# First batch of a pooled attention: half of v loaded in rows of eight tokens and summed by GpSimd instead of TensorE

## The chip, the cores and the metric

The kernel runs on one core of one Trainium2 chip. The metric is the device time of one execution in microseconds (us). Lower is better. The engines are named as in the profile: PE is TensorE (PEld its weight loads), DVE is VectorE, ACT is ScalarE, POOL is GpSimd, SP is SyncE, which here only issues transfers (DMAs). A q behind the name is the engine's sequencer, which waits and issues.

## The reference

Eight batches of attention with eight heads, 576 tokens and 64 columns a head. Keys and values are first averaged over groups of eight tokens, so that 576 queries meet 72 keys. The result of all heads, 4608 rows of 512, goes through a two-layer network with 2048 hidden columns:

```python
k_p = k.reshape(B, H, Sp, pool, D).mean(axis=3)
v_p = v.reshape(B, H, Sp, pool, D).mean(axis=3)
scores = scale * np.matmul(q, k_p.transpose(0, 1, 3, 2))
scores = scores - np.max(scores, axis=-1, keepdims=True)
attn = np.exp(scores)
attn = attn / (np.sum(attn, axis=-1, keepdims=True) + 1e-09)
attn_out = np.matmul(attn, v_p)
...
h = x @ w_in                      # x: attn_out as 4608 x 512
s = np.sin(alpha * h)
g = h + s * s / (alpha + 1e-09)
out = g @ w_out
```

All inputs and the output are float32.

## The kernel before

**Stages.** Both matrix products of the network are done by a fast scheme with seven block products in place of eight (combinations of blocks of w_in and of x are formed first, products p = 1 to 7 follow, and sums put them together). The first layer runs over nine units `u` of 512 rows. Each unit is 28 slots: four groups `J` of seven products, one product a slot (`hidden`, L834, in groups of eight matmuls of 128x256). Its result g goes to a DRAM buffer. The second layer (`outputs`, L1312) reads it back.

**What runs beside it.** `carry(u)` puts the attention of batch u + 1 and other work into the slots of unit u by hand, as a list of functions for each slot. The engines work in the order in which the instructions are written; there is no planner. A DMA issued on SyncE waits in SyncE's own order too, and its rows queue behind those of the DMAs issued earlier.

**The first batch** has its own code (`first_batch`, L1061 and on). Nothing covers it, so the loads of k, q, v and w_in are issued in the order of need, and the sums over eight tokens are split between engines:

- k (`load_k_heads`): four tokens lie in a row; VectorE or GpSimd adds the two halves of a row, and TensorE multiplies by a matrix of ones (`twos`) that also adds and transposes (L374).
- v (`load_v_rows`): heads 0 to 7 lie in a tile `h` of 128 partitions, four tokens of a head to a row of 1 KB, loaded in two DMAs of four heads (L184). `sum_v_rows(b, g, i)` sums heads 4g to 4g + 3 on TensorE: sixteen matmuls with `twos` (L203) into PSUM bank i, and ScalarE copies the result to the tile `vm` (L204). The last 64 tokens of each head are a small DMA of their own (L182), summed with `eights` (L193).
- `a_head(g, ...)` transposes the normalised weights of heads 4g to 4g + 3 on TensorE (L466, L474). `norm_head(hp, eng)` makes them for two heads: a sum and a reciprocal on VectorE (L432, L433), and two multiplications on `eng` (L438). `values` multiplies weights and v (L556, L558), ScalarE scales the result into x (L527) and VectorE forms the first two differences that the fast scheme wants (L567).
- `root` takes an approximate square root for the factor c of s * s; `refine` is one step of refinement, four operations on 128x16 (L644, L645). Squares use c (L991).
- `combine_w_in(J, steps, eng)` forms the combinations of w_in's blocks for group J (L675): step 0 is s1 = a21 + a22, step 1 is s2 = s1 - a11, steps 2 and 3 follow.

Later batches load v otherwise (`load_v`, L140): rows of eight tokens, 2 KB each, heads 0 to 3 into partitions 0 to 63 and heads 4 to 7 into 64 to 127, and GpSimd sums them by halving a row three times (`pool_rows`, L131).

**Order around the change.** In `first_batch` the DMAs on SyncE stand in this order: alternating heads of k and q, v's last tokens, v of heads 0 to 3, v of heads 4 to 7, q of heads 6 and 7, four blocks of w_in (L669), q's last tokens (L101), batch 1's k (L121) and q (L84, L101). Unit 0 follows, with w_in's blocks for groups 1 to 3 in slot 2 and batch 1's v in slot 7. A DMA's completion semaphore comes from a ring of eight, so each issue also waits for the landing of the one eight before it. In slot 1 of unit 0, v of heads 4 to 7 is summed (`sum_v_rows(0, 1, 2)`), q's last tokens are transposed (`rest_q`, L399, into the PSUM bank from which L567 has read) and `a_head(1)` follows; slot 2 has `values` for heads 4 to 7. Batch 1's weights are divided by GpSimd (`norm`, L365), transposed by VectorE (`turn`, L491, L494), and the sums of unit 0 (`hidden`'s adds, L809 and L1036) stand between them in VectorE's order.

Of the kernel before, what the change touches and what calls it, by code (L numbers as in the profile page):

```python
# [19 lines left out]
P = 128  # L20
POOL = 8
# [19 lines left out]
class Kernel:  # L41
# [137 lines left out]
    def load_v_rows(self, b, main, rest):  # L179

        self.v_rows = main.rearrange("p (h t d) -> p h t d", h=self.H, t=4), rest[:64].rearrange("p (h d) -> p h d", h=self.H)
        self.nc.sync.dma_start(out=self.v_rows[1], in_=self.v[b, :, 4 * P:, :].rearrange("h p d -> p h d"))  # L182
        for h in range(0, self.H, 4):
            self.nc.sync.dma_start(out=self.v_rows[0][:, h:h + 4].rearrange("p h t d -> p h (t d)"),  # L184
                                   in_=self.v[b, h:h + 4, 0:4 * P, :].rearrange("h (p t) d -> p h (t d)", t=4))
        self.vp[b] = self.ap.tile([P, self.H // 2, self.D], F32, name="vm", bufs=2), self.ap.tile([P, self.H // 2, self.D], F32, name="vz", bufs=2)

    def sum_v_rest(self, b, i):

        nc = self.nc  # L190
        ps = self.psum([P, 2, self.D], i)
        for hp in range(4):
            nc.tensor.matmul(ps[32 * hp:32 * hp + 32], self.eights[:], self.v_rows[1][:, 2 * hp:2 * hp + 2], start=True, stop=True)  # L193
        nc.vector.tensor_tensor(out=self.vp[b][1][:, 0:2], in0=ps, in1=self.mask[:, 0:2].unsqueeze(2).to_broadcast([P, 2, self.D]), op=OP.mult)
# [866 lines left out]
    def first_batch(self):  # L1061

        nc = self.nc
        self.att = [self.attention(b) for b in range(self.B)]
        A = self.att[0]

        far = [self.home(i, [P, 4 * POOL * self.D]) for i in (1, 2)]
        h = [self.hp.tile([P, 4 * POOL * self.D], F32, name="h") for _ in range(2)]
        self.k_rows = far[0][:].rearrange("p (h t d) -> p h t d", h=self.H, t=4)
        self.k_sums = far[1][:, 0:1024].rearrange("p (h u d) -> p h u d", h=self.H, u=2)  # L1070
        self.new_q(0)
        self.load_alpha(self.hp.tile([P, P], F32, name="s", bufs=1)[:])
        self.load_q_heads(0, 0, 2, nc.scalar)
        add_k = [self.load_k_heads(0, nc.sync, nc.vector)]
        add_rest = self.load_k_rest(h[1][:, 576:832], far[1][:, 1024:1152])
        one = self.sm.tile([P, 1], F32, name="one")
        nc.scalar.activation(out=one[:], in_=self.ident[:, 0:1], func=AF.Sqrt)

        def fill(n):

            for _ in range(n):
                nc.tensor.matmul(self.psum([P, 4, P], 4), self.full[:], self.full[:].unsqueeze(1).to_broadcast([P, 4, P]), start=True, stop=True)
        fill(5)
        self.turn_alpha()
        refine = self.root()
        nc.scalar.activation(out=one[:], in_=one[:], func=AF.Exp)
        add_k[0]()
        tr = self.new_tr()
        nc.gpsimd.memset(tr[:, 2048:], 0.0)
        self.a0 = tr[:, 0:2048].rearrange("p (t j s k) -> p t j s k", t=4, j=4, s=2)  # L1090
        self.z0 = tr[:, 2048:2560].rearrange("p (t hp x k) -> p t hp x k", t=4, hp=4, x=4)
        self.kb2 = h[1][:, 0:self.H * self.Sp].rearrange("p (h k) -> p h k", h=self.H)
        self.a4 = self.last[:64, 0:512].rearrange("p (j s k) -> p j s k", j=4, s=2)
        self.z4 = self.last[:64, 512:640].rearrange("p (hp x k) -> p hp x k", hp=4, x=4)
        nc.gpsimd.memset(self.z4, 0.0)
        for hp in range(1, 4):
            add_k.append(self.load_k_heads(hp, nc.sync, nc.vector if hp < 2 else nc.gpsimd))
            if hp < 3:
                self.load_q_heads(0, 2 * hp, 2 * hp + 2)
        self.load_v_rows(0, h[0][:], self.tp.tile([P, self.DM], F32, name="p5")[:])  # L1100
        self.load_q_heads(0, 6, 8)
        self.load_w_in()
        self.load_w_in_part(0)
        self.q_rest = self.A[3][:64, 0, 512:1024].rearrange("p (h d) -> p h d", h=self.H)
        A.new_a()
        fill(4)
        A.k_head(0)
        add_rest()
        A.q_head(0)
        A.k_last()  # L1110
        for f in add_k[1:]:
            f()
        fill(1)
        A.products_head(0)
        A.q_head(1)
        A.k_head(1)
        A.soft_shift(0)
        A.soft_exp(0)
        fill(1)
        A.products_head(1)  # L1120
        A.k_head(2)
        A.q_head(2)
        A.soft_shift(1)
        A.soft_exp(1)
        A.norm_head(0, nc.gpsimd)
        A.norm_head(1, nc.vector)
        fill(2)
        A.products_head(2)
        self.sum_v_rest(0, 0)
        self.sum_v_rows(0, 0, 3)  # L1130
        A.k_head(3)
        A.q_head(3)
        A.soft_shift(2)
        A.a_head(0, (1, 7, 0), (0,))
        self.combine_w_in(0, (0,), nc.gpsimd)
        A.products_head(3)
        A.a_head(0, (1, 7, 0), (1,))
        A.soft_exp(2)
        A.soft_shift(3)
        A.norm_head(2, nc.gpsimd)  # L1140
        A.soft_exp(3)
        A.norm_head(3, nc.gpsimd)
        self.combine_w_in(0, (1,))
        self.combine_w_in(0, (2, 3), nc.gpsimd)
        A.values((0, 1), (5, 6), 2, 0)
        refine()
        self.load_q_rest(0, self.q_rest)
        for e in range(2):
            self.load_k(1, e)
            self.pool_k[e]()  # L1150
        self.load_q(1)
        self.load_w_in_part(1)

    def carry(self, u):

        nc = self.nc
        x = defaultdict(list)
        at = lambda slot, f, *a: x[slot].append(lambda: f(*a))
        last = self.B - 1
        b = u + 1  # L1160
        if u == 0:
            A0, A = self.att[:2]
            at(1, self.sum_v_rows, 0, 1, 2)
            at(1, A0.rest_q)
            at(1, A0.a_head, 1, (5, 7, 2))
            at(2, A0.values, (2, 3), (2, 1), 1, 1)
            at(2, A0.score, 4)
            at(2, self.sums_of_x, 0, 2)
            at(2, self.sums_of_x, 0, 3)
            at(2, self.load_w_in_part, 2)  # L1170
            at(2, self.load_w_in_part, 3)
            at(2, self.pairs_q, 1, range(5))
            at(4, self.combine_w_in, 1, (0, 1, 2, 3), self.nc.gpsimd)
            at(4, A.q_t, 0, self.nc.vector.tensor_copy)
            at(4, A.q_t, 1, self.nc.vector.tensor_copy)
            at(4, A.k_t)
            at(7, self.load_v, 1)
            at(7, lambda: self.pool_v())
            for i in range(2):
                at((5, 10)[i], A.two_scores, i)  # L1180
            at(13, A.two_shifts)
            for i in range(2, 5):
                at(5 + i, A.q_t, i)
            at(9, A0.exp, 4)
            for i in range(4):
                at((9, 9, 15, 15)[i], A.exp, i)
                at((10, 10, 16, 16)[i], A.norm, i)
                at((13, 13, 17, 19)[i], A.turn, i)
            at(8, self.combine_w_in, 2, (0, 1, 2, 3), self.nc.gpsimd)
            at(13, A0.norm_rest)  # L1190
            at(17, self.combine_w_in, 3, (0, 1), self.nc.gpsimd)
            at(17, self.combine_w_in, 3, (2, 3), self.nc.gpsimd)
            at(23, A0.a_rest)
            at(24, lambda: A0.values_rest((5, 6, 7, (self.turn + 1) % 5)))
            for r in (32, 96):
                at(3, self.nc.gpsimd.memset, self.aM[r:r + 32, :, 704:736], 0.0)
            at(19, A.move, range(3))
            at(20, A.move, (3,), nc.scalar, (0,))
            at(21, A.move, (3,), nc.scalar, (1,))
            at(26, A.all_values)  # L1200
            at(9, self.load_q, 2)
            at(23, self.inner_w_in)
            for e in range(2):
                at(12, self.load_k, 2, e)
                at(17, lambda e=e: self.pool_k[e]())
            at(27, self.att[2].k_t)
            turn = 23
        else:
            at(0, self.sums_of_x, u, 2)
            at(0, self.sums_of_x, u, 3)  # L1210
        if 0 < u < last:
            A = self.att[b]
# [366 lines left out]
```

## Time and profile before

| | before |
|---|---|
| time of a run, median of 3 (lowest to highest) | 905.44 us (905.04 to 906.93) |
| span of the profiled execution, first to last instruction | 902.6 us |
| difference between the two, around the span | 2.84 us |
| TensorE busy in the span | 895.0 us (99%) |
| VectorE, ScalarE, GpSimd busy | 677.4, 448.3, 210.5 us |
| granted TensorE clock | 1.000 |
| mean rate of all transfers over the span | 156 GB/s |
| the same from 2.5 to 40.5 us | 284 GB/s |

The profile tells one execution, in us from its first instruction. Its own time is known as the span; the runs' times also contain what lies around it. A group line gives engine, source line, operation, tile written and tile read, the count, and the busy time. A timeline line begins with start and length. "[0.67 <-POOL ex L365]" means that the engine was idle for 0.67 us before the instruction, and that GpSimd's L365 ended it. The DMA share is the mean busy share of the sixteen DMA engines; it can pass 1, as transfers overlap at their ends.

### The profile page before, as it was taken

To read this page: it belongs to the slowest core of one execution; us is meant where nothing else is said; L and a number is where in the kernel's file an instruction comes from. 1 tells how busy PE (TensorE), PEld (TensorE's weight loads), DVE (VectorE), ACT (ScalarE), POOL (GpSimd) and SP (SyncE) were. 2 spreads that over 40 slices of the span, in tenths; PEclk is the share of its full clock that TensorE was granted. 3 is DMA by queue.
4 is the path that set the end of the run, shared out by engine and by line. 5 is a ranking of instruction groups with operands and counts; after the bars stand their busy time and mean duration, and the time that the engine had idled before them with its cause. 6 is when DMAs were issued, how large, how long until landed. Compare 5 with 4: busy or idle time off the path is not lost.

```text
span 902.6 us, 17941 instructions
## 1 busy us (share of the span) xinstructions
PE 895.0 (99%) x7014; PEld 815.8 (90%) x7014; DVE 677.4 (75%) x1011; ACT 448.3 (50%) x1070; POOL 210.5 (23%) x216
## 2 busy tenths in 40 slices
PE   8999999999999999999999999999999999999998
PEld 5787888888888888888888999999999999999997
DVE  7685766768577685764458799979798888889895
ACT  5696776877768778687976611111111111111111
POOL 4788552824438253430000000000000000000000
PEclk9999999999999999999999999999999999999999
DMA  9965867759586595648216346261618162534401
GB/s 261 245 200 158 220 163 202 196 167 251 139 213 186 177 230 143 176 146 293 93 72 227 102 141 199 59 194 38 224 27 230 33 197 67 172 92 127 137 15 40
DMA packets 128747, 141.13 MB, mean 156 GB/s; under 512 B 46920, under 2 KB 95704, under 8 KB 128664
## 3 DMA queue, kind: packets, MB, share of 16 engines
q1 hardware_dynamic: 125880, 137.88, 53.2%
q10 hardware_dynamic: 2784, 2.11, 0.9%
q8 instruction: 56, 0.92, 0.4%
q14 instruction: 27, 0.22, 0.1%
HBM read 75.37 MB, written 47.19 MB: 136 GB/s over the span
## 4 chain that ended last, share of the span: by engine, by line
PE 91%; DMA 3%; DVE 2%; POOL 2%; SPq 1%; issue 0%; ACT 0%; DVEq 0%; POOLq 0%
PE PS L834 42%; PE PS L1312 41%; PE PS L1014 3%; PE PS L308 2%; PE PS L600 2%; DMA a<-in_moe_w_in_dram 2%; DMA kvin<-in_v_dram 1%; SPq L669 1%; PE PS L613 1%; DVE x L1267 1%; DMA h<-in_k_dram 1%; POOL kvin L131 0%; POOL as L675 0%; DVE s L1267 0%; POOL ex L365 0%
## 5 line engine op out<-in xcount | busy, mean ns | idle before, releaser
L834 PE MATMUL PS<-home,a 128*128 128x256 f32 x1104 | 257.9, 381 | 0.7 <-ACT home L527 0.5
L834 PEld LDWEIGHTS PS<-home,a 128*128 128x128 f32 x1104 | 205.2, 190 | 34.1 <-issue 5.0
L834 PE MATMUL PS<-home,as 128*128 128x256 f32 x768 | 183.0, 382 | 0.0
L834 PEld LDWEIGHTS PS<-home,as 128*128 128x128 f32 x768 | 141.6, 190 | 19.8 <-ACT PS L810 1.2
L1312 PE MATMUL PS<-s,wb 128*128 128x144 f32 x896 | 119.1, 286 | 0.0
L1362 POOL TENSOR_TENSOR cc<-cc,cb 128x576 f32<-128x576 f32 x1 | 2.0, 1976 | 501.8 <-DVE cb L1267 501.8
L1312 PEld LDWEIGHTS PS<-s,wb 128*128 128x128 f32 x896 | 113.7, 190 | 0.1
L991 ACT ACTIVATE s<-s,c 128x256 f32<-128x256 f32 (+1 forms) x228 | 113.5, 564 | 0.0
L809 DVE TENSOR_TENSOR h<-PS,p 128x512 f32<-128x512 f32 x72 | 49.2, 683 | 64.2 <-PE PS L834 36.3
L131 POOL TENSOR_TENSOR kvin<-kvin 96x768 f32<-96x768 f32 (+3 forms) x42 | 71.6, 1705 | 69.5 <-DMA kvin<-in_v_dram 67.9
L1440 ACT COPY PS<-PS 128x144 f32<-128x144 f32 x56 | 14.7, 263 | 145.0 <-PE PS L1312 135.5
L984 ACT ACTIVATE s<-h,al 128x256 f32<-128x256 f32 x144 | 65.6, 510 | 39.4 <-DVE h L809 39.3
L1312 PE MATMUL PS<-r,wb 128*128 128x144 f32 x512 | 73.3, 286 | 0.3 <-DVE r L1267 0.3
L1312 PE MATMUL PS<-s,a 128*128 128x144 f32 x512 | 73.2, 286 | 0.0
L1036 DVE TENSOR_TENSOR h<-PS,s 128x512 f32<-128x512 f32 x36 | 24.7, 687 | 59.8 <-ACT s L991 59.8
L984 ACT ACTIVATE s<-PS,al 128x256 f32<-128x256 f32 x144 | 60.1, 470 | 18.6 <-PE PS L834 17.7
L1312 PEld LDWEIGHTS PS<-r,wb 128*128 128x128 f32 x512 | 67.1, 190 | 0.5 <-DVE r L1267 0.5
L1312 PEld LDWEIGHTS PS<-s,a 128*128 128x128 f32 x512 | 67.1, 190 | 0.0
L810 ACT COPY PS<-PS 128x512 f32<-128x512 f32 x72 | 41.5, 576 | 35.0 <-PE PS L834 30.4
L1460 ACT COPY PS<-PS 128x144 f32<-128x144 f32 x56 | 14.7, 263 | 88.1 <-PE PS L1312 88.1
L1312 PE MATMUL PS<-s,we 128*128 128x144 f32 x384 | 54.9, 286 | 0.0
L1312 PE MATMUL PS<-x,wb 128*128 128x144 f32 x384 | 54.9, 286 | 0.0
(215 smaller groups left out, 1407.7 us busy)
## 6 DMA issues: line engine op xcount, KB each, us to landing
g_bridge<-h SPq DMA_DIRECT2D x72, 512.0 KB
r<-g_bridge SPq DMA_DIRECT2D x31, 1152.0 KB
out_dram<-o SPq DMA_DIRECT2D x122, 72.0 KB
kvin<-in_k_dram SPq DMA_DIRECT2D x14, 576.0 KB
q<-in_q_dram SPq DMA_DIRECT2D x7, 1024.0 KB
kvin<-in_v_dram SPq DMA_DIRECT2D x14, 512.0 KB
aM<-tr SPq DMA_DIRECT2D x54, 92.0 KB
aM<-tr SPq DMA_DIRECT2D x54, 88.0 KB
```

Of the source, the lines that this page charges most:

```text
L131: self.nc.gpsimd.tensor_tensor(out=t[..., 0:w] if w > D else out, in0=t[..., 0:w], in1=t[..., w:2 * w], op=OP.add)
L308: nc.tensor.matmul(ps[e][r0 + r:r0 + r + q.shape[-1], h, :], q[s], kb[s, hp, :], start=True, stop=True)
L600: nc.tensor.matmul(o[r:r + 64], w, x, start=start and i < 2, stop=False, skip_group_check=True)
L809: add = lambda o, x, y: nc.vector.tensor_tensor(out=o, in0=x, in1=y, op=OP.add)
L810: copy = lambda o, x: nc.scalar.copy(out=o, in_=x)
L834: nc.tensor.matmul(ps[:, jj, :], self.A[p][:, kk, f * P:(f + 1) * P], x[:, kk, :], start=(start and n == 0), stop=(kk == 1), skip_group_ch ...
L984: self.nc.scalar.activation(out=G.s[:, i, jj, j, :], in_=src[:, jj], func=AF.Sin, scale=self.al[:, f:f + 1])
L991: self.nc.scalar.activation(out=x, in_=x, func=AF.Square, scale=self.c[:, f:f + 1])
L1014: nc.tensor.matmul(o, W[m][:, G.J - J0], X[m], start=start and n == 0, stop=True, skip_group_check=True)
L1036: add = lambda o, x, y: self.nc.vector.tensor_tensor(out=o, in0=x, in1=y, op=OP.add)
L1312: nc.tensor.matmul(out, W[:, J // 2, J % 2, :], A[:, J, :], start=(start and J == 0), stop=(J == self.NJ - 1), skip_group_check=True)
L1440: nc.scalar.copy(out=x1[:, 0, :], in_=x0[:, 1, :])
```

## The change

For the first batch, v of heads 4 to 7 is no longer part of `load_v_rows`. A new function `load_v_eights` loads it into the second half of the same tile in rows of eight tokens: two DMAs, heads 4 and 5 into partitions 0 to 63 and heads 6 and 7 into 64 to 127, issued behind q of heads 6 and 7. It returns a function that sums on GpSimd straight into `vm`; that stands in the order ahead of the first w_in combination. `sum_v_rows(0, 1, 2)` in slot 1 is gone. The division of heads 6 and 7 moves from GpSimd to VectorE. `values` for heads 0 to 3 now stands ahead of the combination s2, so on VectorE the differences come first. `refine` moves from the end of `first_batch` to slot 1 of unit 0, behind `a_head(1)`.

```diff
@@ load_v_rows
-        for h in range(0, self.H, 4):
-            self.nc.sync.dma_start(out=self.v_rows[0][:, h:h + 4].rearrange("p h t d -> p h (t d)"),
-                                   in_=self.v[b, h:h + 4, 0:4 * P, :].rearrange("h (p t) d -> p h (t d)", t=4))
+        self.nc.sync.dma_start(out=self.v_rows[0][:, 0:4].rearrange("p h t d -> p h (t d)"),
+                               in_=self.v[b, 0:4, 0:4 * P, :].rearrange("h (p t) d -> p h (t d)", t=4))
...
+    def load_v_eights(self, b, x):
+
+        x = x.rearrange("p (h x) -> p h x", h=2)
+        for s in range(2):
+            h = 4 + 2 * s
+            self.nc.sync.dma_start(out=x[64 * s:64 * s + 64], in_=self.v[b, h:h + 2, 0:4 * P, :].rearrange("h (p t) d -> p h (t d)", t=POOL))
+        return lambda: self.pool_rows(x, self.vp[b][0][:, 2:4])
@@ first_batch
         self.load_q_heads(0, 6, 8)
+        add_v = self.load_v_eights(0, h[0][:, 2 * POOL * self.D:])
         self.load_w_in()
...
         A.a_head(0, (1, 7, 0), (0,))
+        add_v()
         self.combine_w_in(0, (0,), nc.gpsimd)
...
-        A.norm_head(3, nc.gpsimd)
+        A.norm_head(3, nc.vector)
+        A.values((0, 1), (5, 6), 2, 0)
         self.combine_w_in(0, (1,))
         self.combine_w_in(0, (2, 3), nc.gpsimd)
-        A.values((0, 1), (5, 6), 2, 0)
-        refine()
+        self.refine = refine
@@ carry, u == 0
-            at(1, self.sum_v_rows, 0, 1, 2)
             at(1, A0.rest_q)
             at(1, A0.a_head, 1, (5, 7, 2))
+            at(1, self.refine)
```

## The prediction

> **What bounds the kernel now.** I read the page first. TensorE is busy for nearly the whole span:
>
> ```profile
> PE 895.0 (99%) x7014; PEld 815.8 (90%) x7014; DVE 677.4 (75%) x1011; ACT 448.3 (50%) x1070; POOL 210.5 (23%) x216
> ```
>
> By that line alone a microsecond off TensorE would be a microsecond off the end. The second view is the chain of waits of the first 70 us, since the change lies in the first 26 us and must carry its gain past everything that follows. Columns are start and length in us.
>
> ```profile
> 33.76 10.48 DMA kvin<-in_v_dram
> ...
> 44.37 2.37 POOL kvin L131
> 46.74 0.07 issue
> 46.80 2.15 POOL kvin L131
> ...
> 57.11 2.23 POOL ex L365 x2
> 59.34 0.02 issue
> 59.36 0.71 DVE tr L491
> ...
> 66.04 0.59 DVE h L809
> 66.63 0.04 issue
> 66.67 3.50 PE PS L834 x15
> ```
>
> The reader is to see that TensorE, though "99% busy", is held at 66.67 us by something that is not TensorE: a VectorE add (L809), queued behind VectorE's transposes (L491), which wait for GpSimd's divisions (L365), which stand in GpSimd's order behind the pooling of batch 1's v (L131), which starts when that v has landed at 44.24 us. GpSimd is idle for 6.1 us before it and works without a break from 44.37 to 59.33. Its matmul before that started at 66.18 and they are spaced by 0.22 us, so it loses some 0.27 us there. Two chains arrive there almost together. If TensorE comes earlier and the other does not, TensorE waits; if the other comes later, everything after does, since from there to the end TensorE runs without a wait longer than 0.3 us.
>
> Third, why v lands at 44.24: the windows (length, busy time of each engine, clock, DMA share, GB/s).
>
> ```profile
> core 0: us, PE busy (x) PEld busy (x) DVE busy (x) ACT busy (x) POOL busy (x), PEclk, DMA share, GB/s
> 12.00:15.00 3.00, 2.90 (x63) 2.42 (x64) 2.90 (x8) 1.17 (x4) 1.74 (x2) 1.00 1.10 349
> 30.00:33.00 3.00, 3.00 (x16) 2.62 (x15) 2.97 (x5) 3.00 (x7) 2.73 (x5) 1.00 1.10 346
> 36.50:40.50 4.00, 4.00 (x49) 3.46 (x42) 3.90 (x9) 1.17 (x4) 1.79 (x2) 1.00 1.05 181
> ```
>
> The DMA share is above 1 in all three, and 1.09 over 2.5 to 40.5 us as a whole: the transfers queue, so whatever lengthens one of them delays all that are issued behind it, batch 1's v among them. The same view gives the price. Rows of 1 KB into 128 partitions (12 to 15 us, this very v among them; w_in in 30 to 33) move at 346 to 349 GB/s. In 36.5 to 40.5 the queue holds batch 1's v, loaded in rows of eight tokens: two transfers of 64 partitions each, 2 KB a row. It moves at 181.
>
> **The change, part by part.** *Loads.* One transfer of 512 KB for heads 4 to 7 (128 partitions, 1 KB a run) becomes two of 256 KB (64 partitions each, 2 KB a run), the form of L140. They are put behind q of heads 6 and 7, which lands sooner; TensorE turns that q at 14.69 us right after other work, so this brings nothing. SyncE issues one more DMA (0.60 us each at L140, with twice the rows); behind it stand w_in part 0, q's rest, batch 1's k and q, w_in parts 1 to 3 and batch 1's v. The issue is covered by the queued transfers; without that cover it costs 0.6. The transfer itself is not covered: 524 KB take 1.50 us at 349 GB/s and 2.90 at 181, so +1.40. Bounds: 0 if the halves mix on the queue so that their rows go at the full rate (2 KB runs might then even gain 0.1), and above, +2.1 from the slow tail (third rival). I take 1.40: L140 is the same form, in a queue just as full.
>
> The Trainium skill, page "SBUF — State Buffer", section "Door 1: The DMA port swizzle", says that partitions 0 to 63 reach only half of the ports that 128 partitions reach, and gives 196 GB/s against 328 for 1 MiB. An estimate by its figures is 2.7 − 1.6 = +1.1 us, which would make the sum 906.5. The trace agrees in kind, 181 against 346.
>
> *TensorE.* The 16 matmuls of the sum go:
>
> ```profile
> 21.90 1.09 PE L203 MATMUL PS<-h,twos 128*64 128x128 f32 x16
> 22.93 0.46 PE L399 MATMUL PS<-ident,as 64*128 64x64 f32 x4
> ```
>
> ```profile
> 20.46 0.94 DVE L675 TENSOR_TENSOR as<-as,a 128x512 f32<-128x512 f32 x1
> 21.32 0.74 DVE L567 SCALAR_TENSOR_TENSOR home<-PS,home 128x256 f32<-128x256 f32 x2
> ```
>
> The first fence is TensorE's timeline, the second VectorE's. From 21.90 to 22.93, 1.03 us of TensorE's stream, and ScalarE's copy of the result, 0.27. But the next matmuls (L399) write the bank that the differences (L567) read. These end at 22.06 now. VectorE gets the division of heads 6 and 7 ahead of them, in place of the sum L675: 0.84 + 0.31 us (L438 at 13.89) instead of 0.94, so 0.2 later at equal contention, 22.3, and TensorE goes on at 22.4 instead of 22.93: 0.5 gained. Bounds: 1.0 if VectorE is no hindrance, and a loss of 0.4 if its division waits out a GpSimd instruction, as the 128x16 operation at 22.88 did (1.19 us beside a GpSimd sum of 1.26, against 0.22 for one at 22.62).
>
> *GpSimd.* Three adds of 512, 256 and 128 elements: 1.28 (L675) + 0.73 + 0.45 (L131 and its vr form) = 2.5 us, in the 3.27 us that GpSimd idles before 18.15 waiting for w_in. That idle time ends later still, as w_in comes 1.4 later, at about 19.5. Queued behind the adds are the first w_in sum and the division of heads 4 and 5; both move to the later w_in, not to the adds. Without the cover, 2.5. The division of heads 6 and 7 leaves GpSimd: 1.04 + 0.29, in a stretch that ends by 33 us, so GpSimd only idles longer before 44.
>
> *Refinement.* Its four operations (0.60 + 0.22 + 1.19 + 1.19 = 3.2 us) move behind VectorE's copy at 25.21, into the 2.86 us that VectorE idles before 28.75. The squares need the root first at 35.91 (L991). Nothing; if it overran, 0.3 on differences that TensorE meets at 29.23, which the stall below hides. The s2 sum behind the differences has until 29.23 too: nothing.
>
> *Sum.* TensorE arrives at 66.67 about 0.5 us early, and VectorE's chain 1.4 us late. GpSimd's stretch from 44.37 to 59.33 keeps its length; the one operation that shows contention is L131's 512-element add, 2.15 where 1.28 is usual, beside VectorE's 128x1024 add at 46.10. That may go either way by up to 0.9, and I count 0, as GpSimd still starts first. So TensorE resumes at 66.67 + 1.4, and the 0.5 is lost in that wait. The profiled span of 902.6 becomes 904.0; the 2.84 us by which the median of the runs, 905.44, exceeds it stays: **906.8 us**, 0.15% more. A measurement of this kernel tells about 0.2%, 1.8 us, from no change, so I forecast no change within that, on the slow side.
>
> **The rivals.**
> - *The halves cost nothing.* If the sixteen shares of a transfer run out of step by about the length of one half (0.7 us here, as each half is 256 KB), one share can be in the first half while its neighbour is in the second. For it: these halves are half as long as L140's. Then v lands at 44.24 or 0.1 earlier, VectorE still holds TensorE at 66.67, and the saving on TensorE is eaten: 905.3. Against: L140's second half was issued (33.06 and 33.76) long before the stretch at 181, which it did not lift. The Trainium skill, page "DMA: Bandwidth & Descriptors", section "Rules for kernel authors", also says that two transfers to disjoint partition halves serialize; here the rate of 181 agrees. Chance 0.20.
> - *TensorE's saving goes through.* If the wait at 66.67 gave way, 1.0 us would come off: 904.4. For it: 99%. Against: the unbroken chain above. GpSimd would have to lose its contention of 0.9 too. Chance 0.07.
> - *Slower: the last share.* A transfer has landed when the slowest of its shares has. Batch 1's v starts to move at about 35.5, where the rate leaves 348, and its last share lands at 44.24. In these 8.74 us the windows count 177 GB/s, 1.55 MB, which at 348 would take 4.45: 4.3 too long for the 1.05 MB of half rows among them. Half of it for half the bytes is +2.1: 907.5. It decides as soon as the extra passes 1.81 us. Against: the tail after 40.5 (135 GB/s) comes with an emptying queue, while here w_in keeps all shares fed. Chance 0.25.
> - The forecast, an extra of 0.7 to 1.8: 0.48.
>
> **How the numbers follow.** Slower by over 0.2% (above 907.25) is nearly all of the last-share rival and the top of the forecast's own spread: 0.27. Faster by over 0.2% (below 903.63) is beyond every priced case, since at most 1.03 comes off TensorE: 0.03 for what I do not see. The rest, 0.70, lies within. The forecast's own range is 906.1 to 907.3. The wide one goes down to the passing of most of TensorE's saving, 904.6, and up to the last share with the scatter of the runs (905.04 to 906.93) on it, 908.2.
>
> **What would show it.** Right: no L203 at 21.9; rows of 2 KB at 12 to 17 us and a rate near 180 to 250 GB/s there in place of 349; GpSimd's w_in sum near 19.5 instead of 18.15; L131 on batch 1's v near 45.8 instead of 44.37; TensorE's wait at 66.67 grown to about 2 us and moved to 68. Wrong: L131 still at 44.4 (the halves are free), or the wait at 66.67 gone (the saving went through), or L131 at 46.5 and later (last share). It would also be wrong if TensorE stalled before 60 us, for q's rest or for a division, by more than the 1.6 us that the wait at 66.67 has room for.

## The result, and the profile after

The changed kernel is slower: 907.91 us median (904.42 to 910.73, 22 runs) against 905.26 for the kernel before in runs beside it (904.21 to 907.46, 22 runs). The ratio is 1.0023, with a 95% interval of 1.0015 to 1.0032, so 2.1 us more (1.4 to 2.9). The ratio goes by the averages of the runs, which lie 2.1 us apart; the medians lie 2.65 apart. The forecast was 906.8, 1.4 us more than before. The time is inside the wide range given (904.6 to 908.2), outside the forecast's own narrower one (906.1 to 907.3), and the loss is just past the 0.2% up to which the forecast counted it as no change. The span of the profiled execution went from 902.6 to 904.6 us; its own time was 906.40, which is 1.8 around the span. With 1.8 around it, the 902.6 of before belongs to a run of about 904.4, so that profile showed a run about a microsecond quicker than the median; the profile of after shows one 1.5 us quicker than its own. All positions below compare one profiled execution with another; the runs decide.

The page's first line says as little as it did before: fewer matmuls by 16, the same 895.0 us.

```profile
PE 895.0 (99%) x6998; PEld 815.6 (90%) x6998; DVE 678.1 (75%) x1013; ACT 447.9 (50%) x1069; POOL 212.9 (24%) x217
```

The windows tell where it begins. Line numbers of after are those of before plus 7, from the new function on. Columns: stretch and length in us, busy time and instructions of TensorE, its loads, VectorE, ScalarE and GpSimd, then clock, DMA share and GB/s. First before, then after, over the 4.5 us in which the first batch's v and the first w_in rows move:

```profile
11.50:16.00 4.50, 4.26 (x74) 3.40 (x72) 4.36 (x10) 2.38 (x6) 2.20 (x3) 1.00 1.10 349
```

```profile
11.50:16.00 4.50, 4.26 (x75) 3.31 (x74) 4.36 (x10) 2.31 (x6) 2.29 (x3) 1.00 1.10 222
```

The sixteen DMA engines are as busy as before (1.10) and move 222 GB/s in place of 349. That is (349 − 222) / 349 × 4.5 = 1.64 us of transfer lost in this stretch alone. Later the queue of after even runs short of work. From 30 to 36 us, first before, then after:

```profile
30.00:36.00 6.00, 6.00 (x45) 5.13 (x47) 4.96 (x9) 5.97 (x12) 5.57 (x8) 1.00 1.10 348
```

```profile
30.00:36.00 6.00, 5.92 (x42) 5.06 (x38) 4.69 (x11) 5.22 (x10) 5.65 (x7) 1.00 1.00 321
```

SyncE issued batch 1's v at 35.97 in after and at 33.06 in before. Why it was late can be read from the landing times that the trace keeps. Each transfer lands in sixteen shares, as many as there are DMA engines, and in after one share of each lagged behind the other fifteen from w_in on: for q's last tokens fifteen shares had landed by 20.84 and the last by 23.84 (before: 19.05 and 20.54). Each issue waits for the last share of the transfer eight places ahead of it. In after, w_in's issues at 33.14, 33.83 and 34.51 follow last shares at 33.12, 33.82 and 34.50, whose other fifteen had landed some 1.5 us earlier (31.61, 32.30, 33.02). That fits the DMA share of 1.00: the other fifteen engines ran out of work. The late share isn't a mark of the half rows: it shows in e10 below, which has none (20.78 and 22.92 for q's last tokens, 41.67 and 45.81 for batch 1's v), and less in e1, which has them (20.79 and 21.73, 47.11 and 47.28). What makes a share late isn't known.

On GpSimd, before and then after:

```profile
44.37 4.58 POOL L131 TENSOR_TENSOR kvin<-kvin 128x1024 f32<-128x1024 f32 x2 [6.08 <-DMA kvin<-in_v_dram]
```

```profile
46.27 4.58 POOL L131 TENSOR_TENSOR kvin<-kvin 128x1024 f32<-128x1024 f32 x2 [5.72 <-DMA kvin<-in_v_dram]
```

Batch 1's v, issued some 30 us behind the changed transfer, is pooled 1.90 us later. The chain of waits of after (start, length) shows the end of it, and a second late branch:

```profile
34.29 0.59 POOL kp L131
34.88 0.04 issue
34.92 0.47 PE PS L276 x3
...
57.75 1.27 POOL as L682
59.02 2.23 POOL ex L372 x2
61.24 0.02 issue
61.27 0.71 DVE tr L498
...
67.95 0.59 DVE h L816
68.53 0.04 issue
68.58 3.50 PE PS L841 x15
```

TensorE resumes at 68.58 in place of 66.67, 1.91 us later, and the span is 2.0 longer. From GpSimd's first add on batch 1's v to TensorE's first matmul behind the wait are 22.30 us before and 22.31 after; from there to the end of the span 835.9 and 836.0. So, between these two profiles, the whole loss has been made by 68.58. GpSimd works from 46.27 to 61.2 without a gap, as it did from 44.37 to 59.33. The list of the chain turns off at 57.75 to VectorE's maximum (57.74), because that ended at the same moment as GpSimd's own row before it; it then goes back over TensorE to batch 1's pooled k at 34.29. This is the other branch: TensorE itself is late too. In its timeline:

```profile
20.23 1.99 PE L841 MATMUL PS<-home,a 128*128 128x256 f32 x8 [0.40 <-ACT home L534]
23.97 0.43 PE L406 MATMUL PS<-ident,as 64*128 64x64 f32 x4 [1.75 <-DMA as<-in_q_dram]
...
68.58 2.64 PE L841 MATMUL PS<-home,a 128*128 128x256 f32 x11 [0.70 <-DVE h L816]
```

The 16 matmuls of the sum are gone, but in their place TensorE waits 1.75 us for q's last tokens, which stand in the queue behind the half rows and whose last share was 3 us late. It passes 23.97 where it passed 22.93. At the end it still waits 0.70 for VectorE, so it was ready at 67.88. In before its matmuls ahead of 66.67 ended at 64.67 + 1.89 = 66.56 by the same view. Two branches are late, by 1.9 and by 1.3 us, and the later one counts. The second can't be put down to the half rows alone: in e1 and e5 below, which have the same transfer, q's tokens came in time.

### The profile page after: what moved, and what is told of

Read it like the earlier page. It is cut to its first block, busy times and chain, and to the rows that moved or that the text cites. A ratio compares the mean times of both kernels' runs of the same rounds, so it can differ in the third digit from the quotient of the medians.

```text
span 904.6 us, 17910 instructions
## 1 busy us (share of the span) xinstructions
PE 895.0 (99%) x6998; PEld 815.6 (90%) x6998; DVE 678.1 (75%) x1013; ACT 447.9 (50%) x1069; POOL 212.9 (24%) x217
## 4 chain that ended last, share of the span: by engine, by line
PE 93%; DVE 2%; DMA 2%; POOL 2%; issue 1%; SPq 0%; ACT 0%; POOLq 0%; DVEq 0%
PE PS L841 43%; PE PS L1321 41%; PE PS L1021 3%; PE PS L315 2%; PE PS L607 2%; DMA a<-in_moe_w_in_dram 1%; PE PS L620 1%; POOL kvin L131 1%; DMA q<-in_q_dram 1%; DVE x L1276 1%; DVE s L1276 0%; POOL ex L372 0%; POOL as L682 0%; DVE r L1276 0%; PE PS L276 0%
## 5 line engine op out<-in xcount | busy, mean ns | idle before, releaser
L131 POOL TENSOR_TENSOR kvin<-kvin 96x768 f32<-96x768 f32 (+3 forms) x42 | 73.6, 1752 | 69.2 <-DMA kvin<-in_v_dram 67.6
```

The source lines that it names most:

```text
L131: self.nc.gpsimd.tensor_tensor(out=t[..., 0:w] if w > D else out, in0=t[..., 0:w], in1=t[..., w:2 * w], op=OP.add)
```

## The experiments

Each ratio is to the kernel before on the same chip, with its 95% interval.

**Which part of the change is it?** *e1_v_alone* keeps the half rows and GpSimd's sum, and puts back the rest: `norm_head(3)` on GpSimd, `values` behind s2, the refinement at its old place. *e2_rest_alone* is the kernel before with only that rest changed.

```diff
 e1, against after
-        A.norm_head(3, nc.vector)
-        A.values((0, 1), (5, 6), 2, 0)
+        A.norm_head(3, nc.gpsimd)
...
-        self.refine = refine
+        A.values((0, 1), (5, 6), 2, 0)
+        refine()
...
-            at(1, self.refine)
```

> The v part of the change alone (loads in half rows, sum on GpSimd, no sum on TensorE); division of heads 6 and 7, values and refinement stand as before. Theory (half rows hold up the transfer queue, batch 1's v lands later, and GpSimd, VectorE and then TensorE wait for it): batch 1's v is pooled (L131) near 46.3 instead of 44.4, and the time is 1.5 to 2.5 us over the kernel before, like the full change. Rival (the moved division and the new order on VectorE cost it): L131 near 44.4 to 45 and within 0.7 us of the kernel before.

> The other three edits alone (division of heads 6 and 7 on VectorE, values ahead of s2, refinement later); v is loaded and summed as before. Theory (half rows): L131 stays at 44.4 and the time within 0.5 us of the kernel before. Rival (order on VectorE): 1.5 to 2.5 us over.

e1: 907.93, 1.0030 (1.0018 to 1.0041). e2: 905.73, 0.9997 (0.9985 to 1.0009). The whole loss is in the part that concerns v (half rows, GpSimd's sum, 16 matmuls fewer); division, order and refinement cost nothing that can be measured. TensorE's timeline of e1 and then of e2, at the place of the wait:

```profile
68.83 3.58 PE L841 MATMUL PS<-home,a 128*128 128x256 f32 x10 [2.28 <-DVE h L816]
```

```profile
67.70 3.72 PE L834 MATMUL PS<-home,a 128*128 128x256 f32 x16 [0.87 <-DVE h L809]
```

In e1 q's tokens came in time, and TensorE passed L406 at 22.37, 0.56 us earlier than before; yet at the end it was ready at 68.83 − 2.28 = 66.55, against 66.56 before. Its saving had gone on the way (e9 shows where), and v, pooled at 47.41, held it for 2.28 us more. e2 has the rate of before (349 GB/s) and still resumes at 67.70, with v pooled at 45.42: one profiled execution scatters by a microsecond in v's landing, without any change in the loads.

**Which property of the half rows?** Against before they differ in three things: 2 KB rows in place of 1 KB, two transfers in place of one, 64 partitions each in place of 128. *e3_halves* is the kernel before with the same 1 KB rows in two transfers of 64 partitions; *e4_heads* has two transfers too, each of two heads over all 128.

```diff
 e3, against before
...
+        for s in range(2):
+            r = slice(64 * s, 64 * s + 64)
+            self.nc.sync.dma_start(out=self.v_rows[0][r, 4:8]..., in_=self.v[b, 4:8, 256 * s:256 * s + 256, :]...)
 e4, against before
...
+        for h in range(4, self.H, 2):
+            self.nc.sync.dma_start(out=self.v_rows[0][:, h:h + 2]..., in_=self.v[b, h:h + 2, 0:4 * P, :]...)
```

> The kernel before, with the one load of v of heads 4 to 7 split into two transfers of 64 partitions each; rows stay 1 KB, place, sums and everything else stay. Theory in its strict form (64 partitions are what slows the queue, whatever the row's length): L131 near 46, time 1.5 to 2.5 us over the kernel before. Rival A (the rows of 2 KB are what slows it): L131 at 44.4 to 44.8, time within 0.5 us.

> Control for the split above: the same load split into two transfers of two heads each, each over 128 partitions. Theory (64 partitions): L131 within 0.4 us of 44.4 and time within 0.5 us of the kernel before. Rival (one more DMA in the ring of eight semaphores, or its issue, is the cost): as slow as the split by partitions, 1.5 us and more.

e3: 906.98, 1.0025 (1.0010 to 1.0039). e4: 906.21, 1.0001 (0.9990 to 1.0012). The windows of e3 and then of e4 in the same stretch:

```profile
11.50:16.00 4.50, 3.80 (x68) 2.71 (x67) 4.36 (x10) 1.97 (x5) 1.86 (x3) 1.00 1.13 269
```

```profile
11.50:16.00 4.50, 4.26 (x75) 3.31 (x74) 4.36 (x10) 2.12 (x6) 2.67 (x4) 1.00 1.10 350
```

The second transfer costs nothing, and the longer rows aren't needed for the loss: 64 partitions with 1 KB rows lose as much as the whole change, within the intervals. e3's twelve runs fall into two halves, six from 905.3 to 906.2 and six from 907.8 to 910.8, so its median is only 1.1 us over before and its loss doesn't come in every execution; the profiled one is of the quick half. One expectation failed: e4's v was pooled at 46.65, not near 44.4, later than in after. But its time and its rate are those of before. So single landings scatter by some 2 us, and one profile's landing must not be read as the effect of an edit. What carries the conclusion is the runs: with half rows in this place (after, e1, e3) 0.23 to 0.30% over before, without them (e2, e4, and e11 below) within 0.03%. The Trainium skill, page "SBUF — State Buffer", section "Can I just issue two DMAs to hit both halves?", says no: two transfers at partitions 0 and 64 serialize. Here 222 and 269 GB/s against 350 agree.

**Is it the wait for batch 1's v?** *e5_after_v1_early* is the changed kernel with the loads of batch 1's v issued in slot 2, ahead of w_in part 3, and pooled in slot 7 as now. *e8_before_v1_early* is the same edit on the kernel before.

```diff
 e5, e8
             at(2, self.load_w_in_part, 2)
+            at(2, self.load_v, 1)
             at(2, self.load_w_in_part, 3)
...
-            at(7, self.load_v, 1)
             at(7, lambda: self.pool_v())
```

> The changed kernel, with the DMAs of batch 1's v issued in slot 2 ahead of w_in's last blocks (group 3) instead of in slot 7; GpSimd pools it in slot 7 as before. Theory (TensorE is held near 68 us through batch 1's v, GpSimd and VectorE): the pooling starts near 42 to 43 instead of 46.3, TensorE's wait near 68 goes, and the time drops by 0.8 to 1.5 us below the changed kernel, not more, since TensorE itself is some 1.2 us late there from its wait for q's last tokens at 24 us. Rival (that chain is only a bystander): no change from the changed kernel, 907.5 to 908.5.

> The kernel before, with batch 1's v issued in slot 2 as above. Theory: TensorE's wait at 66.7 us (0.3 us in the first profile, but about as much more in slower runs as batch 1's v lands later) goes: 0.5 to 1.5 us below the kernel before, with less spread between runs. Rival (bystander): within 0.3 us of the kernel before.

e5: 904.84, 0.9994 (0.9982 to 1.0007). e8: 905.43, 1.0004 (0.9995 to 1.0013). With v ahead of w_in the loss is gone, 2.6 us of it counted from the changed kernel, more than the 0.8 to 1.5 expected. In e8 the same edit brings nothing, where 0.5 to 1.5 was expected. So v's lateness alone is not what before's runs hang on; that TensorE's own branch comes up against the same moment would explain it, but no run shows it by itself. The profiles don't show v much earlier either: it is pooled at 44.64 in e5, where 42 to 43 was expected, and at 44.57 in e8, where one share of it was late by 2.1 us (42.33 and 44.44). In e5 the wait at the end has gone, and TensorE is held earlier, by something else:

```profile
23.53 0.46 PE L410 MATMUL PS<-ident,as 64*128 64x64 f32 x4 [1.58 <-DVE home L578]
...
67.30 3.62 PE L845 MATMUL PS<-home,a 128*128 128x256 f32 x16
```

These are the differences, which the forecast put at 22.3. VectorE's division in front of them (L449, two instructions) took 2.26 us here and 1.90 in after, where the two from L438 at 13.89 in before took 1.07. In after and e5 a w_in sum and a division of GpSimd's ran beside it; in before only a division (13.14 to 14.88).

**Can the transfer be put where it hurts less?** *e6_after_eights_later* issues the half rows behind w_in part 0 and q's last tokens, and GpSimd's sum moves down, behind the division of heads 4 and 5 and ahead of the last two combinations of w_in. *e7_after_both* is e5 and e6 together.

```diff
 e6, against after
-        add_v = self.load_v_eights(0, h[0][:, 2 * POOL * self.D:])
         self.load_w_in()
         self.load_w_in_part(0)
...
+        self.load_q_rest(0, self.q_rest)
+        add_v = self.load_v_eights(0, h[0][:, 2 * POOL * self.D:])
...
+        add_v()
         self.combine_w_in(0, (2, 3), nc.gpsimd)
```

> The changed kernel, with the two transfers in half rows issued behind w_in part 0 and q's last tokens, and their sum on GpSimd moved behind the division of heads 4 and 5. Theory: TensorE's wait at 24 us for q's last tokens goes, but batch 1's v is still pooled at 46 or later, so the time stays within 0.7 us of the changed kernel. Rival (the wait at 24 us for q's last tokens is what costs): 1.2 us or more below the changed kernel.

> Both moves together. Theory: with neither wait left TensorE's saving of 1.0 us comes through: 2 to 4 us below the changed kernel and 0.5 to 1.5 below the same move in the kernel before. Rival (another engine is behind these two): no better than the kernel before with batch 1's v early.

e6: 905.50, 1.0007 (0.9998 to 1.0015). e7: 905.75, 1.0009 (1.0000 to 1.0017). e6 recovers most of the loss, some 1.5 us, against what was expected of it: that is what its rival said (the wait for q's tokens is what costs). It doesn't prove the rival, since v was pooled at 45.00 there and not at 46 or later, so both waits had eased at once. e7 recovers no more than e6 and none of TensorE's saving. In e6 q's tokens no longer stop TensorE, but what GpSimd now does later does:

```profile
34.95 0.47 PE L276 MATMUL PS<-ident,kp 96*128 96x96 f32 x3 [0.78 <-POOL kp L131]
```

That is batch 1's pooled k, ahead of which GpSimd's moved adds now stand. e6 also bounds what the half rows cost: the same two transfers, five issues later, still move ahead of batch 1's k, q, w_in and v, and the kernel is only 0.6 us over before (0.2 less to 1.4 more). Why the place matters so much is not shown. e7's profile is a poor witness: it is one of its longest runs (907.13), and from 2.5 to 12 us its granted clock was 0.82 where before had 1.00, so its first product began at 21.89, 1.9 us later than before.

**What is TensorE's saving worth by itself?** *e9_no_sum* is the kernel before without the sum of v for heads 4 to 7 (that part of `vm` is zero), so without its 16 matmuls; *e10_no_sum_v1_early* adds the early load of batch 1's v.

```diff
 e9, against before
+        nc.gpsimd.memset(self.vp[0][0][:, 2:4], 0.0)
...
-            at(1, self.sum_v_rows, 0, 1, 2)
```

> The kernel before without TensorE's sum of v for heads 4 to 7 (left out; that part of the pooled v is filled with zeros by GpSimd in idle time). All loads stay. What TensorE's 1.03 us are worth by themselves. Theory (the next matmuls wait for VectorE's differences, and the chain through batch 1's v stands right behind): 0 to 0.5 us below the kernel before. Rival (TensorE alone sets the end): 0.9 to 1.1 us below.

> The same, with batch 1's v issued in slot 2 ahead of w_in's last blocks. Theory: with the chain behind it loosened, a further 0 to 0.5 us, so 0.3 to 0.8 below the kernel before; not the full 1.03, since VectorE's differences still end at the same time. Rival: as above.

e9: 905.22, 0.9994 (0.9984 to 1.0005). e10: 904.21, 0.9984 (0.9975 to 0.9993). Taking 1.03 us from TensorE brings nothing that can be told from zero, but the interval (1.4 us less to 0.5 more) does not exclude the whole 1.03 either; with v early it brings 1.4 us (0.6 to 2.3). TensorE's timeline of e9 shows where part of the 1.03 goes:

```profile
22.44 0.46 PE L399 MATMUL PS<-ident,as 64*128 64x64 f32 x4 [0.15 <-DVE home L567]
...
33.67 0.47 PE L269 MATMUL PS<-ident,kp 96*128 96x96 f32 x3
```

From the first product (20.29) to L399 are 2.15 us, against 2.95 before; to L269, which turns batch 1's pooled k, 13.38 against 13.68. Of the 0.80 saved at L399, 0.30 is left; 0.26 of the 0.5 lost is a wait for k at the end. GpSimd's rows of the pooling say why, first of before, then of e9:

```profile
28.72 2.89 POOL L131 TENSOR_TENSOR kvin<-kvin 96x768 f32<-96x768 f32 x2
31.69 0.92 POOL L131 TENSOR_TENSOR kp<-kvin 96x192 f32<-96x192 f32 x1
```

```profile
29.04 3.91 POOL L131 TENSOR_TENSOR kvin<-kvin 96x768 f32<-96x768 f32 x2
33.03 0.58 POOL L131 TENSOR_TENSOR kp<-kvin 96x192 f32<-96x192 f32 x1
```

The two adds took 1.02 us longer, k was ready at 33.61 in place of 32.61, and TensorE, which had 1.05 us in hand here (33.66), had none left. VectorE's two sums beside them (L804) show the other side, before and e9:

```profile
31.12 1.04 DVE L804 TENSOR_TENSOR home<-home 128x512 f32<-128x512 f32 x1
32.09 1.08 DVE L804 TENSOR_TENSOR home<-home,home 128x512 f32<-128x512 f32 x1
```

```profile
30.81 0.68 DVE L804 TENSOR_TENSOR home<-home 128x512 f32<-128x512 f32 x1
31.41 0.68 DVE L804 TENSOR_TENSOR home<-home,home 128x512 f32<-128x512 f32 x1
```

In before VectorE's sums begin 2.40 us after GpSimd's adds and are the ones that lose; in e9 they begin 1.77 after, run at 0.68 each, and GpSimd loses the microsecond. Other kernels split by the same lead: 1.78 us in after, 1.76 in e1, 1.85 in e11 and 2.06 in e5, all with VectorE at 0.67 and GpSimd's two adds at 3.91 to 4.20. In e2, at 2.87, they meet GpSimd's last short add, which takes 1.64 in place of 0.58. In e6 and e7, at 0.78 and 0.80, both lose: VectorE's sums take 1.58 and 1.48 or 1.49 us, GpSimd's adds 3.23. So it is the exact meeting that counts, and not simply a shorter lead. TensorE sets when VectorE's sums come (L558 releases them by way of the differences), and GpSimd's adds on k follow its w_in sums without idle time; TensorE early, or GpSimd late as in after, makes the lead short. In after it is this k at which the chain of waits stands at 34.88. That the lead decides is read from these rows; no run moved L804 by itself.

**A way without half partitions.** *e11_four* keeps the load of before. GpSimd adds the four tokens in each row, and TensorE joins two rows with 4 matmuls in place of 16. *e12_four_v1_early* is that with v early.

```diff
 e11, against before
+    def add_v_rows(self):
+        x = self.v_rows[0][:, 4:8]
+        add = lambda o, a, b: self.nc.gpsimd.tensor_tensor(out=x[:, :, o], in0=x[:, :, a], in1=x[:, :, b], op=OP.add)
+        add(slice(0, 2), slice(0, 2), slice(2, 4))
+        add(0, 0, 1)
...
-        for t in range(4):
+        last = 0 if g else 3
+        for t in range(last + 1):
...
         A.a_head(0, (1, 7, 0), (0,))
+        self.add_v_rows()
```

> The kernel before; v of heads 4 to 7 keeps its load over 128 partitions, GpSimd adds the four tokens of a row (two operations, 2.0 us, in its idle time before the first w_in sum), and TensorE only joins two rows: 4 matmuls instead of 16, so 0.77 us less on TensorE, with no half rows. Theory (half rows are the whole cost of the change): within 0.6 us of the kernel before, on the fast side. Rival (taking the sum to GpSimd is itself what costs): 1 us and more over.

> The same, with batch 1's v issued in slot 2: the version that should be best. Theory: 0.2 to 0.9 us below the kernel before. Rival: not below it.

e11: 905.59, 0.9998 (0.9987 to 1.0009). e12: 904.59, 0.9981 (0.9972 to 0.9989), which is 1.7 us less than before (1.0 to 2.5), and better than both kernels. Three rows of e12, the first two TensorE's, the last GpSimd's:

```profile
34.27 0.47 PE L281 MATMUL PS<-ident,kp 96*128 96x96 f32 x3 [0.15 <-POOL kp L131]
...
67.06 3.62 PE L846 MATMUL PS<-home,a 128*128 128x256 f32 x16
```

```profile
43.70 3.71 POOL L131 TENSOR_TENSOR kvin<-kvin 128x1024 f32<-128x1024 f32 x2 [3.82 <-DMA a<-in_moe_w_in_dram]
```

The last row names w_in, but the last share of v landed at 43.57, so v ended that wait here too. TensorE passes 67.06 without a wait; the small wait for k stays, its pooling at 3.97 us like the others. The saving alone (e9, e11) and v early alone (e8) each bring nothing that can be told from zero; together (e10, e12) they bring 1.4 to 1.7 us. That fits two branches arriving together, but it is argued and not shown. e8 ran on another chip than the other four, with before itself at 905.23 there and 906.14 here, and the size is not explained by the profiles: e12's span is 902.7, before's 902.6. The runs say a little more: those of before on this chip lie from 903.7 to 908.7, those of e12 from 904.0 to 905.9. What e12 takes away is above all the long runs. They may be those in which v came late; no profile shows one of them.

## Why the prediction was right, and where its sizes were off

**What bounds.** Right for the changed kernel: TensorE at 99% was not the bound; the wait behind batch 1's v was, and with v early the loss goes (e5). In before v alone is not the bound, as e8 shows. The distance from v's first add to TensorE's resumption is 22.27 to 22.31 us in before, after, e2, e3 and e4. In e1 it is 21.42, as the first two adds took 3.72 us there and 4.57 or 4.58 in the others: the contention that the forecast left at zero can go by 0.9, but in after it did not.

**The transfer, +1.40: cause right, size somewhat small.** The cause was right, and e3 against e4 shows it, with the other runs on either side: the 64 partitions. The runs put the whole loss at 2.1 us (1.4 to 2.9), so 1.40 lies at the lower edge. The forecast also counted the issue as covered by the queued transfers; in after it was not, as the DMA share of 1.00 from 30 to 36 us shows, where (348 − 321) / 348 × 6 = 0.47 us of transfer were lost (an estimate from the two rows). And the first w_in sum on GpSimd started at 21.03 us in place of 18.15, where 19.5 was forecast:

```profile
16.61 2.09 POOL L131 TENSOR_TENSOR h<-h 128x512 f32<-128x512 f32 x2 [1.37 <-DMA h<-in_v_dram]
18.77 0.46 POOL L131 TENSOR_TENSOR vm<-h 128x128 f32<-128x128 f32 x1
21.03 1.60 POOL L682 TENSOR_TENSOR as<-a,a 128x512 f32<-128x512 f32 x1 [1.81 <-DMA a<-in_moe_w_in_dram]
```

Of the w_in block that ended its wait, fifteen shares had landed by 18.75 and the last by 20.97; in e1, with the same half rows and no such lag, the sum started at 18.83. The rival of the last share gave +2.1 and L131 at 46.5 or later, the forecast 45.8; measured is 46.27, between the two, and its 1.90 is past the 1.8 up to which the forecast went. In this pair of profiles the fifteen shares of batch 1's v came 1.2 us later (45.09 against 43.91) and the last one 1.9 (46.14 against 44.24), so some 0.7 is the late share and the forecast's 1.40 is near the rest. A late last share, as the rival had it, was therefore real in this execution; that half rows make it late is not shown (e10). The forecast had set against it that w_in keeps all shares fed; the share was late with w_in queued behind it. That the two add up to the 1.9 of one execution, near the 2.1 of the runs, is in part luck: without half rows in this place, v was pooled as late as 46.65 (e4). How the loss divides in the other runs is not settled.

**TensorE, 0.5 gained at 22.4: wrong.** TensorE was at L399 at 23.97, 1.04 us later than before. Two hindrances were there. VectorE's division took 1.90 us and not 1.07, so the differences ended at 23.38:

```profile
20.82 1.90 DVE L445 TENSOR_TENSOR tr<-ex,sm 128x512 f32<-128x512 f32 x2
22.64 0.74 DVE L574 SCALAR_TENSOR_TENSOR home<-PS,home 128x256 f32<-128x256 f32 x2
```

And q's last tokens, issued behind the half rows, landed later still, at 23.84. The forecast named both as ways to fail, and gave 0.4 for the division. Its own +1.4 on q's tokens would have made them land at 20.54 + 1.4 = 21.94, in time for 22.4; it was the late share, 3.0 us behind the other fifteen where before had 1.5, that stopped TensorE in this execution. It cost nothing here, for the reason it gave: TensorE had room at the last wait. But the room was nearly used, 0.70 us of it being left. The Trainium skill, page "SBUF — State Buffer", section "Who interferes with whom", says that a VectorE instruction with two SBUF inputs and a GpSimd instruction that reads SBUF exclude each other; the division at 1.90 beside GpSimd's sum and division agrees, and so do L804 and the pooling of k. In before, too, a division of GpSimd's ran beside the 1.07; there it was GpSimd that lost, with 0.74 us for its last part, which takes 0.29 at 22.5. The forecast priced the division at equal contention.

**GpSimd's adds covered, refinement free.** Right. The adds at 16.61 and 18.77 end before w_in comes; in e1 they end just as it comes (18.83). e2 moves the refinement and costs nothing.

**TensorE's saving is lost in the wait.** Right for the changed kernel: e1 waits 2.28 us there. For the saving alone the runs leave room (e9's interval reaches to 1.4 us less). Incomplete in the reason: before it ever reaches the wait at 66.67, 0.5 of the 0.8 that e9 had saved goes by 33.6, half of that on pooled k, whose pooling takes GpSimd a microsecond longer when VectorE's sums meet it otherwise.

**The class.** The price of +1.4 left 0.4 us to the bound of 1.8. The measured +2.1 passes it, and the median, 907.91, lies above the 907.25 over which the forecast gave 0.27. So "no change" turned into a small loss through the size of this one term.

## What to carry to other kernels

In a full queue, a transfer into 64 partitions can be paid by what is issued behind it (1.4 to 2.9 us here); look for the place where it hurts least, since with the same transfers five issues later the kernel lost only 0.6 us (e6). Don't count an issue as covered without asking which landing it waits for. To take matmuls off TensorE is worth something only if each later meeting point (here the differences, pooled k, and v) has room too, counted with VectorE and GpSimd in the order that the earlier TensorE will give them. Where two branches may arrive together, an experiment on one can show nothing; change both, as e12 did, before judging either. And size an effect by many runs: one profile's landing was off by 2 us while the time and the rate were those of before (e4).

## What the runs showed of the hardware that was not expected

- Transfers of 64 partitions with 1 KB rows, among rows of other transfers into 128, moved 269 GB/s over the whole stretch against 350 (e3, e4), with the DMA engines just as busy (1.13 and 1.10).
- A VectorE division of 128x512 in two instructions took 1.90 and 2.26 us beside a w_in sum and a division of GpSimd's (after, e5), against 1.07 beside a division alone (before); and two VectorE sums that began 1.77 instead of 2.40 us after GpSimd's adds took 0.68 instead of 1.04 and 1.08 us, and the adds 3.91 instead of 2.89.
- With the loads untouched, batch 1's v was pooled at 44.37, 45.42, 43.98 and 43.49 in single executions (before, e2, e11, e9), and at 46.65 with one load split without loss of rate (e4).
- Of the sixteen shares of a transfer, one can stay behind the others through many transfers: by 1.3 to 3.0 us in after for the landings from 18 to 43 us, by 1.3 to 4.1 in e10 from 17 to 46, in the transfers that can be followed. In both, issues waited for it, and the DMA share fell (1.00 and 0.99 from 30 to 36 us, against 1.10 in before).
